# A decode step of attention and a token mixer: two weight loads are cut, and four DMA engines carry half of each

## The chip, the cores and the metric

The kernel runs on one core of a Trainium2 chip. The time is device time in microseconds (us) from start to end of one execution, as the median of several runs. A second source is one execution under the hardware profiler, which records every instruction and every DMA packet; its span runs from the first instruction to the last.

## The reference

Two layers, each with an attention block A and a mixer block B, on one token for each of two sequences (B = 2, D = 512). The attention has 32 query heads over 8 key and value heads of 128 with a cache of 32768 positions. Both layers use the same caches and the same weights wq and wo.

```python
def _A_ref(x, k_cache, v_cache, wq, wo):
    q = (x @ wq).reshape(B, Sq, Hq, Dh).transpose(0, 2, 1, 3)
    k = jnp.repeat(k_cache, rep, axis=1)
    v = jnp.repeat(v_cache, rep, axis=1)
    scores = jnp.einsum("bhqd,bhkd->bhqk", q, k) * (Dh ** -0.5)
    p = _softmax(scores, axis=-1)
    o = jnp.einsum("bhqk,bhkd->bhqd", p, v)
    return o.transpose(0, 2, 1, 3).reshape(B, Sq, Hq * Dh) @ wo
...
x = x + _A_ref(_layernorm(x), A_k_cache, A_v_cache, A_wq, A_wo)
x = x + _B_ref(_layernorm(x), B_w1, B_b1, B_w2, B_b2)
x = x + _A_ref(_layernorm(x), A_k_cache, A_v_cache, A_wq, A_wo)
x = x + _B_ref(_layernorm(x), B_w1, B_b1, B_w2, B_b2)
```

All is float32. The block B normalises x over the channels, multiplies by w1 (1792 hidden values per channel), applies a gelu and sums with w2.

## The kernel before, in words

A unit is one layer, one sequence and one key head, `u = (layer, b, h)`. There are 32 units. Each reads 16 MB of keys and 16 MB of values, in 64 groups of 128 x 512 values each. SBUF holds one tile `mem` of 106 cells; a cell takes one such group, 2 KB in each of the 128 partitions. The key step (`k_step`, line 360) multiplies four groups with the query of the unit into the tile `scores`; the value step (`v_step`, line 428) multiplies four groups with the exponentials of the scores into `acc`. Key steps of one unit and value steps of the unit before follow each other as `Order` writes them out; the two places where the layer changes have an order of their own, with loads cut small.

Of the weights, one key head's share of wq and of wo is 1 MB each: 128 rows of 2048 values, so one row of 8 KB for each partition and four cells of `mem`. They lie together in the input `wqo`, for each head 128 rows with the row of wq first and the row of wo behind it. `wide_products` (line 325) reads wq and makes a query, `out_2` (line 492) reads wo. The heads 6 and 7 load their weights once, the heads 0 to 5 once in each layer; with wq and wo that makes 28 weight loads.

The order of all loads is fixed before the program is written. `plan_loads` walks through the steps, keeps a list of what is needed when, and gives each load its cells, its size and the step behind which it is issued. A load of weights is asked for by a step number: `ASK_Q` = 16 steps ahead of the unit's first key step for wq. Its label is `("W", (part, layer, h), 0)`, with part "q" or "o". The function `load` then issues the transfer on SyncE's queue; nearly all loads stand on this one queue, in order, and each waits there for its cells to be free (semaphore of TensorE) and for the loads that it follows (semaphores `DMAHW0` to `DMAHW7`, which are given out in turn, so that a load shares its semaphore with the load eight issues before). ScalarE's queue carries two small inputs at the start and one row of the output (line 592); the last row leaves through SyncE (line 777).

The lines that the change touches are those of `load` (899) and of the host's arrangement of `wqo` (946).

Of the kernel before, what the change touches and what calls it, by code (L numbers as in the profile page):

```python
# [13 lines left out]
P = 128  # L14
# [24 lines left out]
STEP_US = 1.6  # L39
ASK_Q = 16  # L40
ASK_O = 8


class Order:
# [161 lines left out]
def gqa_mixer_kernel(ctx: ExitStack, tc: tile.TileContext, x, kt, v, wqo, cols, out):  # L206
    nc = tc.nc
    B, D = out.shape
    HKV = wqo.shape[0]
    R = wqo.shape[2] // (2 * D)  # L210
    DH = kt.shape[2]
    DT = D // P
    FT = (cols.shape[1] - 2) // 4
    SCALE = DH ** -0.5
    assert DH == P and R * 8 == 32 and DT == NG and R == NG and D == G and B == 2 and R == QT

# [14 lines left out]
    def cells(a, n):  # L231
        return mem[:, a * G : (a + n) * G]
# [9 lines left out]
    half_neg = const.tile([P, 1], F32, name="half_neg")  # L242
    selg = const.tile([P, R * QT], F32, name="selg")
    sel1 = selg[:, 0:1].to_broadcast([P, P])
    keep = const.tile([P, B], F32, name="keep")
    quad = const.tile([P, QT], F32, name="quad")
    head = const.tile([P, R], F32, name="head")
    oz = [const.tile([P, 2 * R + 1], F32, name=f"oz{k}") for k in range(2)]
    qz = const.tile([P, 28 + 32 * SLOTS], F32, name="qz")
# [10 lines left out]
    def quarter():  # L260

        turn[2] += 1
        k = turn[2] % 4
        return misc[:, k * P : (k + 1) * P]

    def constants():
# [6 lines left out]
        nc.vector.tensor_reduce(  # L273
            selg, ident.rearrange("p (g r) -> p r g", g=NG)[:, : R * QT, :], axis=AX.X, op=ALU.add
        )
# [51 lines left out]
    def narrow_products(us, side):  # L327

        n = side.shape[1]
        pt = quarter()  # L330
        for r in range(R):
            nc.tensor.matmul(  # L332
# [461 lines left out]
    for u in order.units:  # L794
        layer, b, h = u
# [11 lines left out]
    for name, us in users.items():  # L807
        k0 = min(first["K", u] for u in us)
        h = name if isinstance(name, int) else name[1]
# [3 lines left out]
        weights.append((k0 - ASK_Q if k0 else -1, ("q", layer, h), max(first["K", u] for u in us) if both else k0))  # L813
        weights.append((k0 if both else v0 + ASK_O, ("o", layer, h), max(end["V", u, 1] for u in us) + 3))

    for u in order.units:
        layer, b, h = u
# [75 lines left out]
    def load(label, n, a):  # L893
        kind, u, g = label
        if kind == "W":
            part, layer, h = u
            w = D * R
            at_w = 0 if part == "q" else w
            nc.sync.dma_start(cells(a, n), wqo[h][:, at_w : at_w + w])
            (wq_sb if part == "q" else wo_sb)[layer, h] = cells(a, n).rearrange("p (t c) -> p t c", t=DT)  # L900
            return
        layer, b, h = u
        src = (kt if kind == "K" else v)[b * HKV + h, g // HALF, :, (g % HALF) * G : (g % HALF + n) * G]
        nc.sync.dma_start(cells(a, n), src)  # L904
        for j in range(n):
            at_cell[kind, u, g + j] = a + j
            if (kind, u, g + j) in order.kept:
                at_cell[order.kept[kind, u, g + j]] = a + j
# [5 lines left out]
    for label, n, a in begin.get(-1, ()):  # L914
        load(label, n, a)
# [4 lines left out]
    for p, (kind, u, g) in enumerate(steps):  # L920
        (k_step if kind == "K" else v_step)(u, g)
        for f, args in hooks.pop(p, ()):
            f(*args)
        for label, n, a in begin.get(p, ()):
            load(label, n, a)
# [3 lines left out]
def _layout(A_x, A_k_cache, A_v_cache, A_wq, A_wo, B_w1, B_b1, B_w2, B_b2):  # L929
    import numpy as np  # L930

    B, HKV, SK, DH = A_k_cache.shape
    D = A_x.shape[-1]
    U = B * HKV
    kt = A_k_cache.reshape(U, 2, NG, 32, 2, 2, 8, 2, 2, DH).transpose(0, 1, 9, 4, 7, 8, 2, 5, 6, 3)
    wq = A_wq.reshape(D // P, P, HKV, -1).transpose(2, 1, 0, 3)
    wo = A_wo.reshape(HKV, -1, DH, D).transpose(0, 2, 1, 3)
    w1, b1, w2 = (a.reshape(P, -1) for a in (B_w1, B_b1, B_w2))
    none = np.zeros_like(w2)
    w2z = np.stack([none, w2], axis=2).reshape(P, -1)  # L940
    cols = [w1, b1, w2z, none[:, :1], np.broadcast_to(B_b2.reshape(1, 1), (P, 1))]
    return {
        "x": np.ascontiguousarray(A_x.reshape(B * (D // P), P).T),
        "kt": np.ascontiguousarray(kt).reshape(U, 2, DH, HALF * G),
        "v": A_v_cache.reshape(U, 2, P, HALF * G),
        "wqo": np.concatenate([wq.reshape(HKV, P, -1), wo.reshape(HKV, DH, -1)], axis=2),
        "cols": np.concatenate(cols, axis=1),
    }

# [24 lines left out]
```

## Time and profile before

| | |
|---|---|
| median of 3 runs | 2498.51 us (2497.92 to 2499.63) |
| profiled execution | 2500.69 us |
| its span | 2498.9 us |
| granted TensorE clock, mean | 0.765 |
| read from HBM | 1063.29 MB, 426 GB/s over the span |
| TensorE busy | 1343.6 us, 54% |
| weight loads | 28 of 1 MB, median 38.5 us from issue to landing |

The page of the profile gives first the busy time of each engine, then the span in 40 slices with the share of time in which the 16 DMA engines worked, then the queues, then the chain of work that ended last, followed back from the last instruction, then the costliest groups of instructions. Answers of the trace give the same for stretches of time, and what SyncE issued when. A load's time "to landing" runs from its issue to the moment in which the last of its DMA engines has reported. Most of such a time is spent in the queue behind earlier loads.

### The profile page before, as it was taken

How to read it: one execution, taken by the hardware profiler on the slowest of the kernel's cores; microseconds unless marked ns; L12 is line 12 of the kernel's file. 1: busy time of each engine (PE TensorE's matmuls, PEld its weight loads, DVE VectorE, ACT ScalarE, POOL GpSimd, SP SyncE). 2: the span in 40 equal slices, each digit the busy share in tenths (PEclk: the TensorE clock that was granted, in tenths of full speed). 3: DMA queues.
4: the chain of work that ended last, by engine and by line, in shares of the span. 5: the costliest groups of instructions: out<-in, count | busy, mean ns of one | idle time of the engine just before them, and what ended most of it. 6: DMA issues, size and time to landing. Idle time of an engine off the chain costs nothing.

```text
span 2498.9 us, 21072 instructions
## 1 busy us (share of the span) xinstructions
PE 1343.6 (54%) x9564; PEld 376.6 (15%) x9564; DVE 211.3 (8%) x600; ACT 187.4 (8%) x582; POOL 5.2 (0%) x18
## 2 busy tenths in 40 slices
PE   3445455545445544556775774555444544464567
PEld 1111111111111111111121221111111111111113
DVE  1000000000000000001110110000000000000012
ACT  0100000000000000001110210000000000000021
POOL 0000000000000000000000000000000000000000
PEclk8777777777777767778887886777777777777788
DMA  9999999999999999999999999999999999999996
GB/s 419 435 435 431 430 435 432 433 427 436 434 431 435 433 431 428 430 432 411 408 429 422 410 429 435 432 430 436 432 434 431 434 436 430 434 427 435 433 432 280
DMA packets 34946, 1064.64 MB, mean 426 GB/s; under 512 B 4133, under 2 KB 4137, under 8 KB 5034
## 3 DMA queue, kind: packets, MB, share of 16 engines
q1 hardware_dynamic: 34568, 1063.27, 99.1%
q8 instruction: 75, 1.23, 0.2%
q14 instruction: 13, 0.11, 0.0%
q10 hardware_dynamic: 290, 0.04, 0.0%
HBM read 1063.29 MB, written 0.00 MB: 426 GB/s over the span
## 4 chain that ended last, share of the span: by engine, by line
DMA 63%; PE 24%; another core or an unknown queue 11%; DVE 1%; issue 0%; ACT 0%; SPq 0%; POOLq 0%; POOL 0%; DVEq 0%; ACTq 0%
DMA mem<-in_v_dram 35%; DMA mem<-in_kt_dram 28%; PE acc L428 13%; PE scores L360 8%; PE misc L332 1%; PE rows L492 0%; PE bcast L325 0%; PE misc L384 0%; PE misc L451 0%; PE misc L657 0%; SPq L904 0%; ACT S L410 0%; PE misc L378 0%; PE misc L471 0%
## 5 line engine op out<-in xcount | busy, mean ns | idle before, releaser
L428 PE MATMUL acc<-mem,S 128*16 128x512 f32 x4080 | 598.9, 719 | 589.9 <-DMA mem<-in_v_dram 581.6
L360 PE MATMUL scores<-mem,qz 128*32 128x512 f32 x4096 | 598.6, 726 | 532.1 <-DMA mem<-in_kt_dram 532.1
L410 ACT ACTIVATE S<-S,neg 128x128 f32<-128x128 f32 x256 | 129.6, 509 | 2213.0 <-DVE S L405 1188.9
L360 PEld LDWEIGHTS scores<-mem,qz 128*32 128x32 f32 x4096 | 142.8, 127 | 915.0 <-issue 819.5
L428 PEld LDWEIGHTS acc<-mem,S 128*16 128x16 f32 x4080 | 127.5, 107 | 904.5 <-issue 818.8
L370 DVE TENSOR_REDUCE mx<-scores 128x1 f32<-128x512 f32 x64 | 44.3, 692 | 797.5 <-PE scores L360 789.7
L405 DVE STREAM_TRANSPOSE S<-scores 128x512 f32<-128x512 f32 x64 | 45.5, 711 | 125.1 <-PE acc L428 125.1
L410 ACT ACTIVATION_READ_ACCUMULATOR S<-S,neg 128x1 f32 x256 | 47.8, 187 | 0.0
L492 PE MATMUL rows<-mem,oz 128*2 128x512 f32 x248 | 44.1, 794 | 0.3 <-DVE oz L481 0.3
L380 DVE TENSOR_REDUCE m<-misc 1x4 f32<-1x128 f32 x32 | 8.9, 279 | 381.4 <-PE misc L378 381.4
L453 DVE RECIPROCAL rl<-misc 128x4 f32<-128x4 f32 x32 | 5.8, 183 | 382.1 <-PE misc L451 382.1
L462 DVE SCALAR_TENSOR_TENSOR row<-acc,quad,row 128x128 f32<-128x128 f32 x96 | 33.7, 351 | 3.4
L460 DVE TENSOR_SCALAR row<-acc,quad 128x128 f32<-128x128 f32 x32 | 11.2, 351 | 172.7 <-PE acc L428 172.7
L481 DVE TENSOR_TENSOR oz<-misc,rl 128x4 f32<-128x4 f32 x32 | 5.2, 162 | 222.8 <-PE misc L471 222.3
L471 PEld LDWEIGHTS misc<-head,row 128*128 128x128 f32 x64 | 14.0, 274 | 52.2 <-issue 38.3
L325 PE MATMUL bcast<-mem,xw 128*32 128x512 f32 x144 | 20.7, 636 | 1.7 <-POOL x_rs L298 1.7
L451 PEld LDWEIGHTS misc<-both,one 128*128 128x128 f32 x64 | 13.8, 271 | 49.7 <-issue 46.8
L471 PE MATMUL misc<-head,row 128*128 128x4 f32 x64 | 16.8, 334 | 7.3 <-DVE row L462 7.3
L332 PEld LDWEIGHTS misc<-selg,row 128*128 128x128 f32 x128 | 17.3, 210 | 19.6 <-issue 10.2
L576 ACT ACTIVATE row<-bcast,bias,scale 128x512 f32<-128x512 f32 x21 | 16.3, 778 | 38.1 <-PE rows L560 16.1
L332 PE MATMUL misc<-selg,row 128*128 128x2 f32 (+1 forms) x128 | 18.7, 268 | 0.8 <-DVE row L317 0.8
L378 PE MATMUL misc<-ident,mxa 128*1 128x128 f32 x64 | 17.0, 360 | 2.0 <-DVE mxa L376 2.0
(137 smaller groups left out, 282.1 us busy)
## 6 DMA issues: line engine op xcount, KB each, us to landing
mem<-in_v_dram SPq DMA_DIRECT2D x13, 4096.0 KB, 25.1
mem<-in_v_dram SPq DMA_DIRECT2D x37, 1024.0 KB, 9.5
mem<-in_kt_dram SPq DMA_DIRECT2D x15, 2048.0 KB, 18.1
mem<-in_kt_dram SPq DMA_DIRECT2D x30, 1024.0 KB, 9.9
mem<-in_wqo_dram SPq DMA_DIRECT2D x28, 1024.0 KB, 38.5
mem<-in_kt_dram SPq DMA_DIRECT2D x6, 4096.0 KB, 29.4
mem<-in_kt_dram SPq DMA_DIRECT2D x2, 6144.0 KB, 25.1
mem<-in_v_dram SPq DMA_DIRECT2D x3, 2048.0 KB, 38.3
```

Source lines behind the costliest of these rows:

```text
L325: nc.tensor.matmul(q_ps[us][32 * d : 32 * d + 32, :], xw[:, d, :], wq[:, d, :], start=True, stop=True)
L332: nc.tensor.matmul(pt[:, r * n : (r + 1) * n], q_row[us][:, r * DH : (r + 1) * DH], side, start=True, stop=True,)
L360: nc.tensor.matmul(sc_ps[u, half][32 * row : 32 * row + 32, :], qz[:, at : at + 32], cells(at_cell["K", u, g], 1), start=(i == 0), stop=(i ...
L370: nc.vector.tensor_reduce(mx[u][:, half : half + 1], sc_ps[u, half], axis=AX.X, op=ALU.max)
L378: nc.tensor.matmul(pm[:1, :P], mxa, ident, start=True, stop=True)
L405: nc.vector.transpose(S[half], sc_ps[u, half])
L410: nc.scalar.activation(s[:, :, h], s[:, :, h], AF.Exp, bias=neg[u][:, h : h + 1], scale=SCALE, accum_out=lsum[u][:, half, h : h + 1],)
L428: nc.tensor.matmul(acc[32 * row : 32 * row + R * QT, :], S[half][:, col : col + R * QT], vc, start=(g < NG), stop=(g >= quads - NG),)
L462: nc.vector.scalar_tensor_tensor(asb[u], acc[:, t * DH : (t + 1) * DH], quad[:, t : t + 1], asb[u], op0=ALU.mult, op1=ALU.add)
L471: nc.tensor.matmul(po_of[u][:, :R], asb[u], head, start=True, stop=(u != order.last))
L492: nc.tensor.matmul(rows[32 * r : 32 * r + B, :], oT[u][:, 2 * r + 1 - b : 2 * r + 3 - b], wo_of(u)[:, r, :], start=False, stop=(u == order ...
L576: nc.scalar.activation(hid[key, f], px[key], AF.Gelu_apprx_tanh, bias=shift[key][:, f : f + 1], scale=slope[key][:, f : f + 1],)
```

## The change

On the host, the 128 rows of each head in `wqo` are put into 32 blocks of four rows, and after each block stands an empty row. So the source of every weight load has three dimensions, 32 blocks x 4 rows x 2048 values, where it was 128 rows x 2048 values. The destination stays 128 partitions.

Two of the wq loads, that of head 5 in layer 0 and that of head 1 in layer 1, are cut. A first transfer brings the partitions 64 to 127 (16 blocks). Four more bring the partitions 0 to 63, each four blocks, that is 16 rows and 128 KB, and each of these runs on four DMA engines.

```diff
+BLOCK = 4
+NARROW = (("q", 0, 5), ("q", 1, 1))
+PIECES = 4
...
-    R = wqo.shape[2] // (2 * D)
+    R = wqo.shape[3] // (2 * D)
...
             at_w = 0 if part == "q" else w
-            nc.sync.dma_start(cells(a, n), wqo[h][:, at_w : at_w + w])
+            size = BLOCK * BLOCK
+            cut = PIECES * size if u in NARROW else 0
+            rows_of = wqo[h][:, :BLOCK, at_w : at_w + w]
+            nc.sync.dma_start(cells(a, n)[cut:, :], rows_of[cut // BLOCK :])
+            for k in range(cut // size):
+
+                nc.sync.dma_start(cells(a, n)[k * size : (k + 1) * size, :], rows_of[k * BLOCK : (k + 1) * BLOCK])
...
+    wqo = np.concatenate([wq.reshape(HKV, P, -1), wo.reshape(HKV, DH, -1)], axis=2)
+    wqo = np.pad(wqo.reshape(HKV, P // BLOCK, BLOCK, -1), ((0, 0), (0, 0), (0, 1), (0, 0)))
...
-        "wqo": np.concatenate([wq.reshape(HKV, P, -1), wo.reshape(HKV, DH, -1)], axis=2),
+        "wqo": wqo,
```

SyncE's queue before, at the first of the two cut loads (the row of `in_wqo_dram` that waits for DMAHW7 is wq of head 5 in layer 0, issued at 679.89 us; the next such row is a wo load). The names in brackets are the semaphores that SyncE waits for.

```order
L904 DMA mem_74<-in_kt_dram 128x16384 [waits DMAHW3_49,PE_49]
L899 DMA mem_74<-in_wqo_dram 128x2048 [waits DMAHW7_49]
L904 DMA mem_74<-in_v_dram 128x16384 [waits DMAHW4_49,PE_49]
L899 DMA mem_74<-in_wqo_dram 128x2048 [waits PE_49]
L904 DMA mem_74<-in_v_dram 128x16384 [waits DMAHW5_49,PE_49]
L904 DMA mem_74<-in_kt_dram 128x16384 [waits DMAHW6_49,PE_49]
L904 DMA mem_74<-in_kt_dram 128x16384 [waits DMAHW0_49,PE_49]
```

The same place of SyncE's queue in the changed kernel:

```order
L913 DMA mem_74<-in_kt_dram 128x16384 [waits DMAHW3_49,PE_49]
L905 DMA mem_74<-in_wqo_dram 64x1x2048 [waits DMAHW7_49]
L908 DMA mem_74<-in_wqo_dram 16x1x2048 x4
L913 DMA mem_74<-in_v_dram 128x16384 [waits DMAHW4_49,PE_49]
L905 DMA mem_74<-in_wqo_dram 128x1x2048 [waits DMAHW5_49,PE_49]
L913 DMA mem_74<-in_v_dram 128x16384 [waits DMAHW6_49,PE_49]
L913 DMA mem_74<-in_kt_dram 128x16384 [waits DMAHW7_49,PE_49]
```

The four pieces take the semaphores 0 to 3, so the loads behind them share a semaphore with younger loads than before: the second V load waits for DMAHW6, that of the K load in the first row, which it did not wait for before, and the K load behind it waits for DMAHW7, that of the piece of 64 rows. At the second cut load the rows of the queue change in the same way. The order of all other loads, and the order on the other engines, stays.

## The prediction

> **What bounds the kernel now.** I read the head of the page first, then its chain that ended last, then the stretches of time by engine, the end of the chain piece by piece, and last SyncE's own queue.
>
> ```profile
> span 2498.9 us, 21072 instructions
> PE 1343.6 (54%) x9564; PEld 376.6 (15%) x9564; DVE 211.3 (8%) x600; ACT 187.4 (8%) x582; POOL 5.2 (0%) x18
> q1 hardware_dynamic: 34568, 1063.27, 99.1%
> DMA 63%; PE 24%; another core or an unknown queue 11%; DVE 1%; issue 0%; ACT 0%; SPq 0%; POOLq 0%; POOL 0%; DVEq 0%; ACTq 0%
> 2300.00:2400.00 100.00, 54.58 (x392) 15.17 (x392) 8.19 (x23) 12.81 (x28) 0.54 (x1) 0.75 1.00 434
> ```
>
> The sixteen DMA engines are at work for 99.1% of the span, TensorE for 54%. The last row is a plain stretch (busy time of PE, PEld, DVE, ACT, POOL, then the clock, the DMA share, GB/s): share 1.00 at 434 GB/s, so one DMA engine moves 434 / 16 = 27.1 GB/s, and one row of 8 KB costs it 8192 / 27.1 = 0.302 us. That is the only price I need, and the bound is the stream of loads on SyncE's queue.
>
> The sixteen do not end together. These are the last loads:
>
> ```profile
> 2474.00:2475.00 1.00, 1.00 (x16) 0.26 (x8) 0.00 (x0) 0.00 (x0) 0.00 (x0) 1.00 1.03 414
> 2475.00:2476.00 1.00, 1.00 (x13) 0.22 (x6) 0.00 (x0) 0.00 (x0) 0.00 (x0) 1.00 0.60 248
> 2476.00:2480.00 4.00, 3.23 (x39) 1.42 (x38) 0.63 (x2) 0.00 (x0) 0.00 (x0) 1.00 0.50 206
> 2481.00:2482.00 1.00, 1.00 (x26) 0.65 (x26) 0.00 (x0) 0.00 (x0) 0.00 (x0) 1.00 0.08 29
> 2482.34 0.04 issue
> ```
>
> The share falls from 1.03 to 0.50 within 2475 to 2476, stays there for 4 us, and the chain's last DMA piece ends at 2482.34, where "issue" takes over. Half of the engines are through about 6 us before the others. Call them the early eight and the late eight. Every load is divided evenly and nothing is consumed until its last engine has landed, so the late eight set the time. What the change does to the time is what it does to the engine that ends last.
>
> An earlier load shows the same spread. These are packets counted in four short stretches; each engine ends a load with one 4-byte packet, which stands under "under 512 B" (q10 is ACT's queue, whose row is stored there; one of the six in the first stretch is its own):
>
> ```profile
> DMA packets 13, 0.40 MB, mean 1318 GB/s; under 512 B 6, under 2 KB 6, under 8 KB 7
> q10 hardware_dynamic: 2, 0.00, 1.9%
> ...
> DMA packets 19, 1.05 MB, mean 428 GB/s; under 512 B 3, under 2 KB 3, under 8 KB 3
> ...
> DMA packets 21, 1.18 MB, mean 347 GB/s; under 512 B 3, under 2 KB 3, under 8 KB 3
> ...
> DMA packets 11, 0.39 MB, mean 655 GB/s; under 512 B 5, under 2 KB 5, under 8 KB 5
> ```
>
> The stretches are 2416.25 to 2416.55, to 2419, to 2422.4, to 2423. Five engines end the V load in the first 0.3 us, three more by 2419, three by 2422.4, five in the last 0.6 us: 5 + 3 + 3 + 5 = 16. First to last is 6.4 us. I take 6.7 us as the lag of the late eight, between this and the end (2482.3 less about 2475.3, 7.0).
>
> **The change part by part.**
>
> *All 28 weight loads get a source of blocks.* Rows stay 8 KB, 128 of them per load, eight per engine, 8 x 0.302 = 2.42 us. I take 0. If the new shape sent rows so that two engines always wrote to one engine's partitions, each load would take twice as long: 28 x 2.42 = 68 us is the far end, a rival below. The gaps are not read, so no bytes are added.
>
> *Issuing.* The sources no longer merge into one dimension, and SyncE takes longer to issue them.
>
> ```profile
> L899 SPq DMA_DIRECT2D mem<-in_wqo_dram x28: 327/423/1450, 0.7 to 2306.6; - x28
> 679.50 0.33 SPq L904 DMA_DIRECT2D mem<-in_kt_dram  x1
> 679.89 0.41 SPq L899 DMA_DIRECT2D mem<-in_wqo_dram  x1
> 699.12 0.33 SPq L904 DMA_DIRECT2D mem<-in_v_dram  x1
> 713.07 0.33 SPq L899 DMA_DIRECT2D mem<-in_wqo_dram  x1
> 718.22 0.33 SPq L904 DMA_DIRECT2D mem<-in_v_dram  x1
> ```
>
> An issue takes 0.33 to 1.45 us, 0.42 at the median, while SyncE issues about once in 14 to 20 us; eight more issues (two loads in five pieces instead of one) are hidden there. Uncovered is only the very first weight load, at 0.7 us, with every other load behind it: 0 to 1.1 us (1.45 - 0.33). I take 0.2.
>
> *A wait that the pieces add.* A load waits for the one eight issues before it on its semaphore. With four more issues, the second V load behind the split weights waits for the K load issued at 679.50, where it waited for an older one.
>
> ```profile
> mem<-in_kt_dram SPq DMA_DIRECT2D x1, 48.0
> mem<-in_wqo_dram SPq DMA_DIRECT2D x1, 1024.0 KB, 50.1
> mem<-in_v_dram SPq DMA_DIRECT2D x1, 50.2
> 757.61 1.04 PE L325 MATMUL bcast<-mem,xw 128*32 128x512 f32 x8
> ```
>
> The K load of 679.50 lands 48.0 us later, at 727.5, so the V load of 718.22 is issued 9.3 us later. Behind it in SyncE's queue stands the next K load; TensorE is the one that would wait. The V load issued at 699.12 lands at 699.1 + 50.2 = 749.3 and its early engines end some 6.7 us before, at 742.6, so 727.5 is still 15 us ahead of the first idle engine: 0 us. If that cover were gone, the price would be up to 9.3 us at each of two places. The weights themselves land at 679.9 + 50.1 = 730.0 and are first used at 757.61: 27.6 us in which a later landing costs nothing.
>
> *The split, twice.* In place of eight rows per engine, the first piece gives its 64 rows to sixteen engines, four each, and the four narrow ones give 64 rows to four engines, sixteen each. The four carry 20 rows, 6.04 us, 3.62 more than before; twelve engines carry 4 rows, 1.21 us, 1.21 less. Total 4 x 20 + 12 x 4 = 128.
>
> That holds if a row costs 0.302 us wherever it lands. But in each load so far an engine fills the same eight partitions; now engines write partitions that belonged to another, which goes on filling them with its own loads. No row of before shows two engines on one engine's partitions. The lower end is 0.302 us; the upper end is twice that, 0.604, if the limit sits where the rows land, with the same 0.302 lost by the owner. The row 2476 to 2480 is the nearest: eight engines left alone move 206 GB/s, 25.8 each, no faster than in company, so the limit is not one that all share; it goes with the engine or with its partitions. I take the upper end, because no row shows the partitions of one engine taking more than 27.1 GB/s. Then, if partitions 0 to 63 are the early eight's and 64 to 127 the late eight's:
> - late eight: own four rows 1.21, and 1.21 lost to the early engines' four rows: 2.42, no gain;
> - the four: 20 rows, of which 4 of the first piece and 8 of the narrow ones land on others' partitions: 6.04 + 12 x 0.302 = 9.66, which is 7.24 more;
> - the other early four: 2.42, and 8 x 0.302 = 2.42 lost to the narrow pieces: 2.42 more, inside their lead of 6.7.
>
> If the four start first among the early eight they end 7.24 - 6.7 = 0.5 us behind the late ones; if one of them is 2.4 us behind the first (the three that ended between 2416.55 and 2419), 2.9. Each split lies ahead of a place where the loads run dry (the change of layer, the end), so it counts in full, twice: 1.0 to 5.8 us. I take the store's engine as the measure, among the first five: 1.0. At the lower price of a row the late eight gain 1.21 and the four, at 3.62 + 2.4 = 6.0, stay level with 6.7 - 1.21 = 5.5: -2.4 us for two, at best.
>
> The Trainium skill, "SBUF — State Buffer", section "Door 1: The DMA port swizzle (why `[64,N]` ≈ `[32,N]`)", says that partitions 0 to 63 hang on only 8 of the 16 ports and gives 196 GB/s for 64 partitions where 128 reach 328. By that rule the rows on others' partitions are shared and the sum is +1.0 or more instead of -2.4; no run shown so far tests it.
>
> Sum: 0 + 0.2 + 0 + 1.0 = 1.2 us. The profiled execution took 2500.69 us (span 2498.9 and 1.8 around it), so it would take 2501.9; the median of the runs, 2498.51, is 2.2 below it, which makes **2499.7 us**.
>
> **The rivals.**
> - *The late eight are relieved*: rows cost 0.302 anywhere. For it: the plain rate per engine is all that the trace shows. Against: two writers on one engine's partitions. 2498.5 + 0.2 - 2.4 = 2496.3.
> - *The four are late ones*, the other side: they end 3.62 us later per split at the low price, 7.24 at the high one: 2505.9 to 2513.2. It decides from the point where one of the four lies within 1.1 us of the last engine: 2 x (3.62 - 1.1) = 5.0. Against it: the one-row store of q10, a data packet and its end packet, so one engine, ran at a moment when the early five were ending and the late ones were 6 us away. The Trainium skill, "DMA: Bandwidth & Descriptors", section "Why a DMA increments its semaphore by 16 and not by 1", says that such transfers take the lowest-numbered engines, as many as divide both sides, so the store's engine would be one of the four; the trace agrees with one engine for one row and shows no numbers.
> - *The pieces are not narrow*: they spread over all engines, and nothing but the issue is left: 2498.7.
> - *Blocks cost every load*: two engines on the same partitions in all 28: 2498.5 + 68 = 2566. Against it: rows, their order and their count per engine stay what they are; nothing in the profile speaks for it.
>
> **How the numbers follow.** Chances: forecast 0.46, late eight relieved 0.27, four late 0.14, not narrow 0.08, blocks 0.03, something unseen 0.02. About 0.2% (5.0 us) is what a measurement of this kernel tells from no change. Relieved, not narrow and the forecast up to 2503.5 lie within it; slower are the four late, the blocks, and the forecast's upper end with two badly placed engines (0.04): 0.21. Faster by that much has no mechanism here: 0.03. The range runs from the relieved case with 0.8 of slack, 2495.5, past the forecast's upper end (2498.5 + 0.2 + 5.8 = 2504.5) to the lower end of the late case, 2506.
>
> **What would show it.** Right: the 1 MB of weights as 512 KB and four of 128 KB; at 2475 to 2482 the DMA share falling in more than one step, with four engines ending as late as the late eight; the chain's last DMA piece ending 0 to 3 us later after each split. The relieved case shows the low plateau shorter by 1.2 us. The late case shows a tail with a share near 0.25 after the others are through. Wrong altogether: a slower rate in every stretch with weights (blocks), or an idle DMA near 743 or 2100 (the added wait).

## The result and the profile after

The changed kernel takes 2508.54 us (median, 2507.70 to 2509.52), the kernel before beside it 2498.16. The ratio is 1.0041 with a 95% interval of 1.0028 to 1.0053, so it is 10.4 us slower. The forecast was 2499.7, with a range from 2495.5 to 2506.

The head of the changed kernel's page, its queue, its chain, and the end of the chain piece by piece:

```profile
span 2507.6 us, 21087 instructions
q1 hardware_dynamic: 34600, 1063.27, 99.1%
DMA 64%; PE 23%; another core or an unknown queue 11%; DVE 1%; issue 0%; ACT 0%; SPq 0%; POOLq 0%; POOL 0%; ACTq 0%; DVEq 0%
2490.52 0.04 issue
```

The bytes are the same (1063.27 MB) and the sixteen DMA engines are as busy as before (99.1% of the span), and yet the chain's last DMA piece ends 8.2 us later, at 2490.52 after 2482.34. So the engines did not wait longer; somewhere they moved less while they were busy. The stretches of time tell where. The columns are the stretch, its length, the busy time of PE, PEld, DVE, ACT and POOL, the granted clock, the DMA share and GB/s. First the changed kernel:

```profile
700.00:720.00 20.00, 11.06 (x74) 2.75 (x74) 1.49 (x4) 2.11 (x8) 0.00 (x0) 0.74 0.99 429
722.00:736.00 14.00, 4.00 (x24) 1.17 (x28) 0.00 (x0) 0.00 (x0) 0.00 (x0) 0.63 0.99 262
740.00:800.00 60.00, 24.62 (x172) 6.97 (x168) 5.25 (x16) 4.23 (x16) 0.00 (x0) 0.71 1.01 434
2078.00:2092.00 14.00, 4.13 (x20) 1.14 (x24) 0.00 (x0) 0.00 (x0) 0.00 (x0) 0.57 1.02 290
2100.00:2160.00 60.00, 28.98 (x192) 8.34 (x196) 4.40 (x14) 4.23 (x16) 0.00 (x0) 0.69 1.01 436
```

Then the kernel before, in the two stretches that stand out:

```profile
722.00:736.00 14.00, 8.35 (x60) 2.54 (x64) 0.00 (x0) 0.00 (x0) 0.00 (x0) 0.64 1.03 442
2078.00:2092.00 14.00, 8.57 (x64) 2.42 (x64) 0.85 (x2) 0.00 (x0) 0.00 (x0) 0.80 0.99 427
```

At each of the two cut loads there are some 14 us with a share of 0.99 to 1.02 and a rate of 262 and 290 GB/s, where the kernel before has 442 and 427. Before and after them the rate is the usual one (429, 434, 436). Put in time at the full rate, 14 x (442 - 262) / 434 = 5.8 us and 14 x (427 - 290) / 434 = 4.4 us. The sum, 10.2, is a rough figure, because packets count where they start. It is of the size of the whole loss: 10.4 us between the medians, 8.8 between the two profiled executions.

The packet records of that stretch say which engines are slow: all of them. The keys and values travel in packets of 64 KB, the weights in rows of 8 KB. All 24 packets of 64 KB that start between 722.6 and 731 us, two for each of the twelve engines that carry any, take 4.0 to 4.6 us where 2.42 is usual. The four narrow engines are on rows of weights in that time, and such a row takes 0.58 us (median) where it was 0.31.

The last loads of the changed kernel:

```profile
2483.00:2484.00 1.00, 1.00 (x13) 0.50 (x9) 0.00 (x0) 0.00 (x0) 0.00 (x0) 1.00 0.74 309
2485.00:2489.00 4.00, 3.71 (x59) 1.83 (x57) 1.32 (x4) 0.00 (x0) 0.00 (x0) 1.00 0.55 220
2489.00:2490.00 1.00, 1.00 (x28) 0.70 (x26) 0.08 (x1) 0.00 (x0) 0.00 (x0) 1.00 0.07 27
```

The share still falls to about one half, stays there for some 4 us and then drops. Eight engines come last, as before. There is no tail at a share of 0.25, in which four would run on alone.

SyncE's queue at the first cut load, and the landings of the weight loads:

```profile
679.88 0.59 SPq L905 DMA_DIRECT2D mem<-in_wqo_dram  x1
680.53 2.80 SPq L908 DMA_DIRECT2D mem<-in_wqo_dram  x4
699.25 0.34 SPq L913 DMA_DIRECT2D mem<-in_v_dram  x1
714.90 0.61 SPq L905 DMA_DIRECT2D mem<-in_wqo_dram  x1
731.93 0.34 SPq L913 DMA_DIRECT2D mem<-in_v_dram  x1
mem<-in_wqo_dram SPq DMA_DIRECT2D x2, 512.0 KB, 54.4
mem<-in_wqo_dram SPq DMA_DIRECT2D x8, 128.0 KB
```

Two loads are cut as the diff says, 512 KB and four of 128 KB, and the V load behind them is issued at 731.93, not 718.22. The row of the 128 KB pieces has no landing time. In the trace each of them has five records on its semaphore, one at the issue and four at its end: four engines. The first piece's four came at 727.2, 727.2, 728.2 and 729.4 us. Of the 512 KB load's sixteen, eight came at 725.5 to 727.5 and eight at 730.6 to 734.1, so the four belong to the early eight.

### The profile page after: what moved, and what is told of

It is laid out like the page before. It is cut to its first block, busy times and chain, and to the rows that moved or that the text cites. A ratio compares the mean times of both kernels' runs of the same rounds, so it can differ in the third digit from the quotient of the medians.

```text
span 2507.6 us, 21087 instructions
## 1 busy us (share of the span) xinstructions
PE 1340.8 (53%) x9564; PEld 376.0 (15%) x9564; DVE 211.2 (8%) x600; ACT 187.6 (7%) x582; POOL 5.2 (0%) x18
## 3 DMA queue, kind: packets, MB, share of 16 engines
q1 hardware_dynamic: 34600, 1063.27, 99.1%
## 4 chain that ended last, share of the span: by engine, by line
DMA 64%; PE 23%; another core or an unknown queue 11%; DVE 1%; issue 0%; ACT 0%; SPq 0%; POOLq 0%; POOL 0%; ACTq 0%; DVEq 0%
DMA mem<-in_v_dram 36%; DMA mem<-in_kt_dram 28%; PE acc L431 12%; PE scores L363 8%; PE rows L495 1%; PE misc L335 1%; PE bcast L328 0%; PE misc L660 0%; PE misc L454 0%; PE misc L387 0%; PE misc L474 0%; DVE row L465 0%; PE rows L749 0%; ACT S L413 0%
## 5 line engine op out<-in xcount | busy, mean ns | idle before, releaser
L335 PEld LDWEIGHTS misc<-selg,row 128*128 128x128 f32 x128 | 17.1, 208 | 18.4 <-DVE rl L456 8.2
L454 PE MATMUL misc<-both,one 128*128 128x4 f32 x64 | 17.0, 336 | 2.0 <-DVE both L453 2.0
```

What stands on the lines that cost most here:

```text
L335: nc.tensor.matmul(pt[:, r * n : (r + 1) * n], q_row[us][:, r * DH : (r + 1) * DH], side, start=True, stop=True,)
L454: nc.tensor.matmul(pl[:, :R], ones, both, start=True, stop=True)
```

## The experiments

Three theories divide the ground.

- **Shared** is the forecast's: two engines that write one engine's usual partitions share its rate, and no other engine is touched.
- **All**: while any engine writes partitions that it does not usually write, all sixteen are slower, at about 0.6 of their rate.
- **Narrow**: a transfer on only four engines is slow in itself.

Which partitions an engine usually writes stands in no record of a trace. The expectation of the second experiment says where the assignment is taken from, and the second and third experiments together test it.

The edits are against the changed kernel. "The loss of a cut" below is what one cut load costs beyond the bytes that it takes from the engines that end last: half of the difference to the kernel before, plus 0.302 us for each row that those engines no longer carry.

### The blocks alone

```diff
-NARROW = (("q", 0, 5), ("q", 1, 1))
+NARROW = ()
```

> The blocks of four rows in all 28 weight loads, and no load is cut. If the split is the whole cause: 2498.2 plus 0 to 1, ratio 1.000. If the blocks cost something in every load (two engines on the same partitions): up to 68 us more; if all of the 10.4 us are theirs, 0.37 us for each load and 2508.5 again.

Measured: 2498.69 us, ratio 1.0002 (0.9992 to 1.0011). The blocks of four rows and the longer issues of 28 loads cost nothing that can be measured. The 10.4 us belong to the split.

### Only the pieces that lie on their engines' own partitions

The cut loads bring partitions 0 to 15 and 32 to 47 alone; the other 96 rows of each are left out.

```diff
-            nc.sync.dma_start(cells(a, n)[cut:, :], rows_of[cut // BLOCK :])
-            for k in range(cut // size):
+            if not cut:
+                nc.sync.dma_start(cells(a, n), rows_of)
+            for k in range(0, cut // size, 2):
```

> Of each of the two cut loads only the narrow pieces of partitions 0 to 15 and 32 to 47 are left; the rows of the other 96 partitions are not loaded. Each of the four engines then carries eight rows as in an ordinary load, the other twelve none. That these are the four engines' usual partitions is taken from the Trainium skill, DMA: Bandwidth & Descriptors, section The descriptor swizzle. Theory 'shared' (two writers share one engine's partitions, nobody else is slowed) and theory 'all' (one engine on another's partitions slows all sixteen): no engine leaves its partitions, so no dip of the rate at 722 to 736; the last engines, which carry nothing, are 2.4 us earlier after each load, 2498.2 - 4.8 = 2493.4. Theory 'narrow' (a transfer on four engines is slow in itself): a dip to some 260 GB/s for 5 us, 2 us lost each, about 2497.

Measured: 2493.31 us, ratio 0.9982 (0.9972 to 0.9992), 4.8 us faster. The stretch of the first cut load:

```profile
722.00:728.00 6.00, 0.61 (x4) 0.23 (x8) 0.00 (x0) 0.00 (x0) 0.00 (x0) 0.62 1.13 487
```

The same stretch of the kernel before:

```profile
722.00:728.00 6.00, 0.35 (x4) 0.23 (x8) 0.00 (x0) 0.00 (x0) 0.00 (x0) 0.50 1.08 459
```

No dip, so four engines are not slow in themselves, and "narrow" falls. (Packets count where they start, so a short stretch can stand above the mean rate.) The gain of 2 x 2.4 us is just the eight rows per load, 8 x 0.302 = 2.42, that twelve engines no longer carry. The four still carry their eight rows, four of each piece, and did not become the last. So the engines that end last set the time, and the four have room.

### The same four engines, on partitions of others

The same again with partitions 16 to 31 and 48 to 63, so the same number of pieces, bytes and engines.

```diff
-            nc.sync.dma_start(cells(a, n)[cut:, :], rows_of[cut // BLOCK :])
-            for k in range(cut // size):
+            if not cut:
+                nc.sync.dma_start(cells(a, n), rows_of)
+            for k in range(1, cut // size, 2):
```

> Of each of the two cut loads only the narrow pieces of partitions 16 to 31 and 48 to 63 are left, on the same four engines; the rows of the other 96 partitions are not loaded. 'Shared': the four and the four owners go at half rate for 4.8 us, (8 + 8/2) x 27.1 = 325 GB/s at that time, the late eight are not touched and gain 2.4 us for each load: about 2493.4. 'All': all sixteen at 0.6 of the rate for 5 us, 260 GB/s, 2 us lost in each place, 2498.2 - 4.8 + 4 = 2497.4. 'Narrow': as e2_own, within 1 us.

Measured: 2499.41 us, ratio 1.0006 (0.9997 to 1.0016): 6.1 us above the run before, from which it differs in the partitions alone. "All" was 2.0 us below it, "shared" 6.0.

```profile
722.00:728.00 6.00, 0.00 (x0) 0.00 (x0) 0.00 (x0) 0.00 (x0) 0.00 (x0) 0.50 0.96 248
```

248 GB/s at a share of 0.96. If only the four writers and the four owners had gone at half their rate, 8 + 8/2 = 12 sixteenths of 434, 325, would be left. In the packet records the four are on their rows of weights from 721.8 to 728.0 us, most of these at 0.63 to 0.66 us. The 64 KB packets that the twelve others start between 721.7 and 724 take 4.4 to 4.9 us, and those that start behind the last row are down to 2.4 to 2.6. Twelve engines are slow, and only four of them can be owners of these partitions. In the run before, no packet of the stretch takes longer than usual. (The source rows differ between the two runs as well; the kernel with the blocks alone reads these rows too, through its sixteen engines, without loss.) The loss of a cut is (2499.41 - 2498.11) / 2 + 2.42 = 3.07 us.

The Trainium skill, "SBUF — State Buffer", section "Door 1: The DMA port swizzle (why `[64,N]` ≈ `[32,N]`)", gives each eight partitions a port that the writers to them share. By that rule alone the eight engines that neither write others' partitions nor have their own written would have kept their rate; the trace disagrees, 248 GB/s instead of the 325 estimated above.

### Only the first piece

Partitions 64 to 127 over sixteen engines; the lower half is left out.

```diff
-            for k in range(cut // size):
+            for k in range(0):
```

> Of each of the two cut loads only the first piece is left, the 64 rows of partitions 64 to 127 on sixteen engines, four rows each; partitions 0 to 63 are not loaded. 'Shared': the late eight save four of eight rows (1.2 us) and lose 1.2 us to the early ones, so no change at the end: 2498. 'All': all sixteen at 0.6 of the rate from the first early engine to the last late one, some 7 to 9 us, 3 to 3.6 lost and 1.2 saved in each of two places: 2502 to 2503. 'Narrow': no dip, 1.2 us saved each: 2495.8.

Measured: 2502.18 us, ratio 1.0015 (1.0006 to 1.0025), slower though half of two loads is missing.

```profile
722.00:730.00 8.00, 0.00 (x0) 0.00 (x0) 0.00 (x0) 0.00 (x0) 0.00 (x0) 0.50 1.06 306
```

The loss of a cut is (2502.18 - 2498.11) / 2 + 4 x 0.302 = 3.24 us. With the 3.07 of the run before that makes 6.31. The changed kernel, which has both and leaves the late engines 4 rows instead of 8, loses 10.38 / 2 + 1.21 = 6.40. So the two parts add up, as closely as such small differences can tell.

### The lower half as one wide piece

No narrow pieces: each cut load in two halves of 64 rows, both over sixteen engines. Every engine carries its eight rows again.

```diff
-            for k in range(cut // size):
-
-                nc.sync.dma_start(cells(a, n)[k * size : (k + 1) * size, :], rows_of[k * BLOCK : (k + 1) * BLOCK])
+            if cut:
+                nc.sync.dma_start(cells(a, n)[:cut, :], rows_of[: cut // BLOCK])
```

> The two cut loads as two pieces of 64 rows, each on sixteen engines, four rows per engine and piece; all rows are loaded, and every engine carries eight, as in an ordinary load. 'All' (an engine on partitions that it does not usually write slows all sixteen): the early eight leave their partitions in the first piece, the late eight in the second some 6 us later, so the rate is low for about 11 to 12 us, 40% of it lost, about 5 us each time: 2508. 'Shared': the late eight lose 1.2 us to the early ones in the first piece and 1.2 us in their own second one: 2503. If the four engines' 20 rows are what costs: no more than 2499.

Measured: 2508.49 us, ratio 1.0040 (1.0025 to 1.0055), the changed kernel's own time.

```profile
722.00:735.00 13.00, 4.29 (x28) 1.24 (x32) 0.00 (x0) 0.00 (x0) 0.00 (x0) 0.61 1.00 255
```

The unequal shares of the engines are not needed for the loss. The loss of a cut is 5.15 us with no engine relieved or burdened.

### Two engines instead of four

The rows of the third experiment (16 to 31 and 48 to 63) in pieces of eight rows, each on two engines.

```diff
-            nc.sync.dma_start(cells(a, n)[cut:, :], rows_of[cut // BLOCK :])
-            for k in range(cut // size):
-
-                nc.sync.dma_start(cells(a, n)[k * size : (k + 1) * size, :], rows_of[k * BLOCK : (k + 1) * BLOCK])
+            if not cut:
+                nc.sync.dma_start(cells(a, n), rows_of)
+            for k in (2, 3, 6, 7) if cut else ():
+                nc.sync.dma_start(cells(a, n)[8 * k : 8 * k + 8, :], rows_of[2 * k : 2 * k + 2])
```

> As e3_foreign, the same 32 rows on the same partitions 16 to 31 and 48 to 63, the rest not loaded, but in four pieces of eight rows: two engines carry sixteen rows each in place of four engines with eight. 'All', as long as any engine is away from its partitions: low rate for 16 x 0.62 = 10 us instead of 5 to 6, so about twice the loss of e3_foreign (3 us each): 2493.3 + 12 = 2505. If the loss goes with the number of rows that land elsewhere: as e3_foreign, 2499.4. If only the two and their two owners are slow: 2493.3, since neither is late.

Measured: 2501.81 us, ratio 1.0015 (1.0005 to 1.0024): a loss of 1.81 + 2.42 = 4.23 us for a cut. "All" had the sign and not the size (2505).

```profile
722.00:732.00 10.00, 0.49 (x4) 0.23 (x8) 0.00 (x0) 0.00 (x0) 0.00 (x0) 0.59 1.10 301
```

301 GB/s over 10 us, against 248 over 6 us with four engines. In the packet records the two are on their rows from 721.9 to 731.6 us. The fourteen that stay on their own partitions start 28 packets of 64 KB between 721.8 and 728, two each, and all 28 are slow: 3.6 to 4.6 us, 4.4 at the median, where four engines away made it 4.8. So two engines slow the others nearly as much as four do, and for longer. With only the owners slowed, this run would have come out at 2493.3. That an engine away from its partitions slows engines that it shares no partitions with is shown; that the factor is always 0.6 is not.

### The lower half on eight engines, each near its own

The first piece as in the change, the lower half in two pieces of 32 rows, each on eight engines.

```diff
-            for k in range(cut // size):
-
-                nc.sync.dma_start(cells(a, n)[k * size : (k + 1) * size, :], rows_of[k * BLOCK : (k + 1) * BLOCK])
+            for k in range(cut // 32):
+                nc.sync.dma_start(cells(a, n)[32 * k : 32 * k + 32, :], rows_of[8 * k : 8 * k + 8])
```

> The two cut loads with the first piece as in the change (partitions 64 to 127 on sixteen engines) and partitions 0 to 63 in two pieces of 32 rows on eight engines, four rows each; all rows are loaded. If the eight engines are the usual ones of these partitions, the second part adds nothing to what e4_upper lost: 2502.2, and 'all' and 'shared' agree on it. If the narrow form costs: as the changed kernel, 2508.5.

Measured: 2505.48 us, ratio 1.0029 (1.0018 to 1.0040), 3.3 us above the first piece alone, where no difference was expected.

```profile
722.00:732.00 10.00, 1.51 (x8) 0.46 (x12) 0.00 (x0) 0.00 (x0) 0.00 (x0) 0.64 1.03 332
```

The eight records at the end of the first piece of 32 rows are at 726.7, 726.7, 727.1, 727.5, 727.5, 727.8, 730.9 and 731.0: six early engines and two late ones. If these eight are the usual engines of partitions 0 to 63, the forecast's "if partitions 0 to 63 are the early eight's" is false for two of them. Those two carry eight rows more than in the run with the first piece alone, up to 2.42 us per cut, of which 3.3 / 2 = 1.65 appear. That this is the cause of the 3.3 us was argued from the records, not tested.

### The two halves, early in the run

The wide halves again, on two weight loads issued at 35 and 201 us in place of the two later in the run.

```diff
-NARROW = (("q", 0, 5), ("q", 1, 1))
+NARROW = (("q", 0, 1), ("q", 0, 2))
```

> As e5_halves (two pieces of 64 rows, nothing left out), but the cut loads are wq of heads 1 and 2 in layer 0, which land near 86 and 246 us, where the engines are still within 1 to 2.5 us of each other, not 5 to 7. If the loss is the time in which any engine is away from its partitions, times some 0.42: 8 rows of 0.62 and the lag of 1 to 2.5, 6 to 7.5 us, 2.5 to 3.2 us lost each: 2503.3 to 2504.5. If each cut costs the same wherever it stands: 2508.5, as e5_halves.

Measured: 2506.06 us, ratio 1.0031 (1.0020 to 1.0042): 4.1 us for each cut, where the same halves cost 5.15 later in the run. It lies between the two expectations. Its interval allows 2.5 to 5.2 us for a cut and so takes in both, so it stays open whether the place in the run matters.

### One cut alone

```diff
-NARROW = (("q", 0, 5), ("q", 1, 1))
+NARROW = (("q", 1, 1),)
```

> The change with the second of its two cut loads alone (head 1 in layer 1). Both cuts cost alike and add up: half of 10.4, 2503.4. If what is lost in layer 0 is partly hidden at the change of layer, the second one alone costs more than half: 2504 to 2508.

Measured: 2503.34 us, ratio 1.0021 (1.0011 to 1.0030), 5.49 us for one cut, a little over half of the 10.38. There is no sign that the two cuts interact.

### Blocks of eight rows

No split; the blocks of all 28 weight loads twice as high.

```diff
-BLOCK = 4
-NARROW = (("q", 0, 5), ("q", 1, 1))
+BLOCK = 8
+NARROW = ()
```

> No load is cut; the rows of all 28 weight loads lie in blocks of eight instead of four (16 blocks), which makes neighbouring eights of partitions go to one engine, by the Trainium skill, DMA: Bandwidth & Descriptors, section Why a DMA increments its semaphore by 16 and not by 1. All loads stay at sixteen engines and eight rows each. 'All': each of the 28 loads opens a low-rate time from the first early engine to the last late one, 5 to 11 us, 2 to 4.5 us lost: 56 to 126 us, so 2554 to 2624. 'Shared': 8 rows at half rate, 2.4 us each, 2565. If the partitions do not matter: 2498.

Measured: 2707.5 us, ratio 1.0827 (1.0808 to 1.0845). This is 209.3 / 28 = 7.5 us for every weight load, more than either theory had. The GB/s in 40 slices of the span, the bytes, and the issues of the weights (count, size, median us from issue to landing):

```profile
GB/s 404 382 435 406 400 431 336 432 394 365 432 338 408 420 304 331 388 397 425 390 424 423 403 429 436 371 433 396 395 433 343 430 399 356 375 403 400 362 424 201
HBM read 1063.29 MB, written 0.00 MB: 391 GB/s over the span
mem<-in_wqo_dram SPq DMA_DIRECT2D x28, 1024.0 KB, 56.9
```

The kernel before:

```profile
mem<-in_wqo_dram SPq DMA_DIRECT2D x28, 1024.0 KB, 38.5
```

Same bytes, same 128 rows on all sixteen engines, and no narrow transfer: some slices fall to 304 to 343, while the best stay at 432 to 436. A weight load takes 18.4 us longer to land. In the semaphore records the first and last engine of one load are up to 30 us apart (775.2 to 805.1), 5.6 before. The very first load, when no engine is ahead of another, takes only some 2.3 us longer (7.5 to 8.7 us for the sixteen, 5.2 to 6.4 before). That is near the 2.4 us of rows at half rate. It fits a price that rises as the engines drift apart, which no run tests by itself. That blocks of eight rows give rows to engines on whose partitions they don't usually lie is worked out from sixteen blocks on sixteen engines and from the likeness to the split; the records of the packets don't name partitions.

## Why the prediction was wrong

- **What bounds the kernel**: right. The engines are at work for 99.1% of the span, before and after, and the eight that end last set the time. The run with the own pieces shows it: 8 rows x 0.302 us off twelve engines, 2.4 us off the run, twice.
- **All 28 weight loads get a source of blocks**, taken at 0: right, 2498.69 with the blocks alone. The rival "blocks cost every load" (2566) is out for blocks of four. With blocks of eight it happened, at 7.5 us a load, three times the 2.42 that the rival allowed for.
- **Issuing**, taken at 0.2: right within what can be measured. An issue takes 0.59 us where it was 0.41.
- **A wait that the pieces add**, taken at 0: it came, and a little later than worked out. The V load is issued at 731.93, 13.7 us later than before and not 9.3, because the K load that it waits for was itself slowed and landed at 731.9. The cover, up to 742.6, held: 434 GB/s at a share of 1.01 in 740 to 800.
- **The split, twice**, taken at 1.0: this is the step that failed. A crossing row is one that an engine writes into partitions that are usually another's. The step put it at 0.604 us "with the same 0.302 lost by the owner", so 1.21 us lost by each late engine and none by engines to which nobody crosses. The runs show that while rows cross, all sixteen engines are slow, the kernel's other loads included: 262 and 290 GB/s in place of 442 and 427. A cut costs the late engines 6.40 us, not 1.21, against the same 1.21 of relief. The row on which the step leaned, 206 GB/s for eight engines left alone, showed that the usual limit is not a shared one; it said nothing about crossing rows, since nothing crosses there. Two smaller things were off in the same step, and neither decides it: the lag of the late eight, taken at 6.7 us, is 5.6 in the kernel before at the first of these loads (724.4 to 730.0), and the lower end of -2.4 has the four "stay level" where its own figures, 6.0 against 5.5, leave them 0.5 behind.
- **If partitions 0 to 63 are the early eight's**: false in part, six early engines and two late ones.
- **The pieces are narrow, and the four are among the early eight**: right, by five records for each piece and by the times at which they end. The Trainium skill, "DMA: Bandwidth & Descriptors", section "Why a DMA increments its semaphore by 16 and not by 1", has the engines be the largest number up to 16 that divides both sides' outer sizes; 16 partitions and 4 blocks make four, and the trace agrees.
- **The rival "the four are late ones"** has the measured time in its range (2505.9 to 2513.2) by luck, for a reason that didn't happen. No four engines stay behind at the end, and the two wide halves, without any narrow piece, give 2508.49.
- **The chances**: 0.21 stood for slower. The case that came true, a loss on every engine, was not among the rivals at all, because the upper end of the unknown price was set by "two share one engine's rate".

## What to carry to other kernels

When a stream of loads is the bound and keeps each DMA engine on the same partitions, a transfer of another shape beside it (half the partitions, fewer engines, a source cut otherwise) can cost far more than its bytes: here 3 to 6 us for 0.25 to 1 MB, on all engines. An unknown price for contention should be bounded above with every engine of the stream paying, not only those that meet. Its mark in a profile is a DMA share that stays at 1.00 while the GB/s drop.

## What the runs showed of the hardware that was not expected

- Two engines of sixteen on partitions that other engines usually write slow the 64 KB packets of the other fourteen from 2.42 to between 3.6 and 4.6 us. In which part of the path they meet stays open, and so does whether it takes the owners writing at the same moment; neither was tried.
- Whether a source with gaps costs nothing or 7.5 us for each MB hangs on the height of its blocks: four rows, ratio 1.0002; eight rows, 1.0827.
- The engines of one queue drift 5.6 to 7 us apart in a steady stream, and up to 30 us with blocks of eight rows. What makes one engine early and another late is open.
